# Turning q and k on TensorE's whole array in place of DMA, in an attention and MLP kernel, with a new order of operations

## The chip, the cores and the metric

The kernel runs on one core of a Trainium2 chip. The metric is the device time of one launch in microseconds; the kernel before has a median of 362.71 us in three runs (362.51 to 363.19). TensorE does the matmuls (its weight loads are recorded apart, as PEld), VectorE (DVE), ScalarE (ACT) and GpSimd (POOL) the rest of the arithmetic, SyncE (SP) issues most of the DMAs.

## The reference

Two layers follow each other. The first is attention without softmax over 8 batches of 12 heads, 448 positions and a head width of 64; the second is an MLP over the 3584 tokens, with 768 inputs and 2048 hidden values.

```python
scores = scale * np.matmul(q, k.transpose(0, 1, 3, 2))
attn = np.maximum(scores, 0.0) ** 2 / S
attn_out = np.matmul(attn, v)
x = attn_out.transpose(0, 2, 1, 3).reshape(B * S, H * D)
h = x @ w_in
g = h * (1.0 / (1.0 + np.exp(-1.702 * h)))
return g @ w_out
```

Inputs and outputs are float32; the kernel computes its products in float16 and sums in float32.

## The kernel before

**Units.** The attention is cut into 24 units, three to a batch, each of four heads. For a unit, q and k are loaded, cast to float16, and turned so that the head width lies on partitions (tiles `qT` and `kT`, 128 x 7 x 128). Then come seven steps of scores (`scores`, L147: four matmuls of 64x64 weights and 448 columns, each in a quarter of the array), relu of each half (`relu`, L158 on VectorE, L160 on ScalarE), the square (L166 on ScalarE, or a product on VectorE), the product with v (`attn_v`, L178: 28 quarter-array matmuls), and two copies of the result to the batch's x (`xb`).

**How q and k are turned.** Units 0 to 5 (batches 0 and 1) are turned by TensorE: `trans_pe`, L128, with two matmuls against the identity for each of seven places, one for each half of the array's columns (`tr`), and `trans_evac` copies the PSUM bank to SBUF on VectorE or ScalarE. Of these, unit 0 is loaded as float32 and cast, and units 1 to 5 are cast by the load itself. Units 6 to 23 are loaded as float32 by SP into a single staging buffer for q and one for k (`load`, L96), cast into an order in which seven squares of 128x128 lie side by side (`cast`), and turned by a DMA that SP issues (`trans_dma`, L116). There are two float16 buffers each for q and for k, and three each for `qT` and `kT`.

**The MLP.** Batch 0 goes through the first matrix in a plain way (`m1`, L214, tile `ht`). Batches 1 to 7 use Winograd's form of Strassen's scheme, with seven products in place of eight (`unit_product`, tile `hx`, 224 columns a matmul, at L194), whose intermediate sums are made by VectorE. Snaps and additions collect the quarters in `gf`, then follow the gelu on ScalarE (L201) and its scaling into `ring` (L204, on POOL or VectorE). The second matrix is applied to pairs of 128-token tiles, again with seven products (`pair_product`, tile `ox`, eight matmuls of 384 columns, at L194). A product's bank is copied or added to the output tile `osb` (`pair_snap`, `pair_last`, L366 on VectorE), which `store` (L306) or `store_part` (L313) writes out by DMA.

**What sets the order.** All operations stand in one long list of words, written out by hand, which the function `do` carries out one after the other. Each engine keeps the order of its own operations in that list, and semaphores order operations of different engines. A word names an operation, its unit or block, the engine after a colon and the PSUM banks after an @: `s6.0@2.3` is step 0 of the scores of unit 6 in banks 2 and 3, `Lk9`, `K9:p`, `Rk9` are load, cast on POOL and DMA turn of unit 9's k, `tk2@1` and `ek2` are turn by TensorE and its copy, `u` is a product `hx`, `p` a product `ox`, `h` and `l` the steps that take it from its bank. PSUM has eight banks, which the words name outright.

The core of the turn by DMA, and the end of the list in the old kernel (tiles 26 and 27 are the last pair; a third number of `p` and `l` is a half of the product's columns):

```python
def trans_dma(n, u):
    t = new(f"{n}T", [128, J, 128], F16)
    nc.sync.dma_start_transpose(
        out=t[:, :, :], in_=units[u].pop(n + "16").rearrange("p j a d -> p (j a d)"))
    units[u][n + "T"] = t
...
            "q26.0.0 l26.3.1 q26.0.1:a l26.3.0 q27.1.0 q27.1.1:a l24.6 o24 p26.5 l26.5 p26.6.0 "
            "l26.6.0 p26.6.1 q27.0.1:a q27.0.0 q26.2.0 q26.2.1:a l26.6.1 q26.3.0 q26.3.1:a"
```

Of the kernel before, what the change touches and what calls it, by code (L numbers as in the profile page):

```python
# [8 lines left out]
F32 = mybir.dt.float32  # L9
# [6 lines left out]
def kernel(  # L16
# [77 lines left out]
    def load(n, u):  # L94
        x = new(f"{n}st", [128, 2, S], F32)
        nc.sync.dma_start(out=x, in_=quad(n, u))  # L96
        units[u][n + "st"] = x
# [6 lines left out]
    def cast(n, e, u):  # L104
        x = units[u].pop(n + "st")
        if u == 0:
            c = new(f"{n}16", [128, 2, S], F16)
            copy(e, c, x)
        else:
            c = new(f"{n}16", [128, J, 2, D], F16)  # L110
            copy(e, c.rearrange("p j a d -> p a j d"), x.rearrange("p a (j d) -> p a j d", d=D))
        units[u][n + "16"] = c

    def trans_dma(n, u):
        t = new(f"{n}T", [128, J, 128], F16)
        nc.sync.dma_start_transpose(  # L116
            out=t[:, :, :], in_=units[u].pop(n + "16").rearrange("p j a d -> p (j a d)"))
        units[u][n + "T"] = t
# [4 lines left out]
    def trans_pe(n, p, u):  # L123
        ps = bank(p, "tr", F16)
        x = units[u].pop(n + "16")
        for j in range(J):
            for a in range(2):
                nc.tensor.matmul(  # L128
                    out=ps[64 * a:64 * a + 64, j * 128:(j + 1) * 128],
                    lhsT=x[:, a, 64 * j:64 * j + 64], rhs=ident[:, :], is_transpose=True)  # L130
        units[u][n + "ps"] = ps
# [176 lines left out]
    def store_part(e, p, m, h, i):  # L308
        b, j = divmod(2 * m + i, J)
        r0 = b * S + j  # L310
        c = slice(h * NOUT, (h + 1) * NOUT) if h < 2 else slice(
            NOUT + NOUT // 2 * (h - 2), NOUT + NOUT // 2 * (h - 1))
        (nc.scalar if e == "a" else nc.sync).dma_start(  # L313
            out=out[r0:r0 + 63 * J + 1:J, c], in_=osb[m][64 * i:64 * i + 64, c])
# [30 lines left out]
    def pair_product(e, p, m, n, h=None):  # L345
        c = (0, 1, 0, 1, 0, 0, 1)[n] if h is None else 2 + h
        if n < 2 or (n == 3 and h is not None):
            op[m, c] = bank(p, "ox")
# [4 lines left out]
        mm(op[m, c][:, k], lambda f: a[:, f, :], lambda f: w[:, f, k], HF, n in (0, 1, 3))  # L353

    def pair_snap(e, p, m, n):
        i, c = {0: (0, lo), 2: (0, hi), 4: (1, hi)}[n]
        copy(e, out_tile(m + i)[:, c], op[m, 0][:, 0:NOUT], 1.0 / SC)

    def pair_last(e, p, m, n, h=None):
        i, c = {1: (0, lo), 3: (1, hi), 5: (1, lo), 6: (0, hi)}[n]  # L360
        o = out_tile(m + i)[:, c][:, quarter(h)]
        if n == 5:
            copy(e, o, op[m, 0][:, 0:NOUT], 1.0 / SC)
        else:
            x = op[m, 1 if h is None else 2 + h][:, quarter(h)]
            nc.vector.scalar_tensor_tensor(out=o, in0=x, scalar=1.0 / SC, in1=o,  # L366
                                           op0=ALU.mult, op1=ALU.add)
# [16 lines left out]
    with tc.manual_schedule():  # L384
# [8 lines left out]
        for n in "kq":  # L393
# [3 lines left out]
            two["R" + n] = lambda e, p, u, n=n: trans_dma(n, u)  # L397
# [22 lines left out]
        def zeros(e, p, n):  # L420
# [8 lines left out]
            "z9@0 z1 z1 jq1 z1 z1 jk1 V1 I Lq0 Lk0 z1 z1 z1 Q0:d tq0@1 eq0:a K0:d tk0@2 tq1@3 ek0 "  # L429
            "eq1 s0.5@4.5 jq2 r0.5.1:d r0.5.0 s0.1@6.7 jk2 s0.2@0.1 r0.2.1 r0.1.1:d jq3 s0.0@2.3 "  # L430
            "s0.3@5.4 r0.1.0 r0.2.0:d r0.3.1 r0.3.0:d s0.4@1.7 tk1@6 ek1 s1.6@0.4 s1.4@5.6 jk3 x0.2 "
            "r0.0.0 V0 r0.4.1 r0.0.1 x0.0 r0.4.0 r1.6.0 s0.6@2.7 x0.3 jwa0 s1.0@3.1 r1.6.1 r1.0.1 "
            "tq2@0 x0.5 eq2 s1.5@4.1 r1.4.1 r1.5.0:d s1.3@0.6 jwb0 r1.4.0 r1.5.1 V2 s1.1@4.5 x1.6 "
            "tk2@1 jq4 r1.3.1 jwb2 x1.4 r0.6.1 ek2 r1.1.1 x0.4 jk4 r0.6.0 jwa2 r1.1.0 r1.0.0 tq3@6 "
            "s2.3@7.1 eq3 x0.1 r1.3.0 r2.3.0 s1.2@5.2 r1.2.1 jwa1 x1.1 jwb1 x0.6 tk3@4 r2.3.1 ek3 "
            "jq5 V3 a0@3.6 r1.2.0 jk5 x1.0 jwb3 x1.2 x1.3:a s2.4@0.7 e0.1:a e0.0:a r2.4.0 s3.3@2.1 "
            "x1.5 r3.3.0:d r3.3.1 r2.4.1:d a1@4.5 e1.0:a V4 e1.1:a s2.2@6.3 r2.2.1:d jwa3 s2.5@0.2 "
            "V5 r2.2.0 x2.3 f0.2.0@1 r2.5.0 jo1.0 s2.0@7.4 r2.0.1 s2.1@5.3 r2.1.1 r2.0.0:d r2.5.1 "
            "f0.2.1 jo0.0 x2.2 f0.3.0@6 r2.1.0:d f0.3.1 x2.0 s2.6@0.4 r2.6.1 r2.6.0 s3.1@3.7 r3.1.0 "
            "s3.0@2.5 r3.1.1:d jo1.1 tq4@4 f0.1.0@0 jo0.1 r3.0.0:d eq4 x2.4 x2.6 x2.1:a f0.1.1 "  # L440
            "s3.2@3.7 x2.5:a r3.2.0 a2@2.4 tk4@3 r3.2.1:d r3.0.1 e2.0:a s3.6@7.5 e2.1 ek4 f0.3.2 "
            "r3.6.0:d x3.2 r3.6.1 f0.2.2 g0.3 g0.2 f0.1.2 g0.1 s3.5@2.4 s3.4@3.7 r3.4.0 r3.4.1 "
            "r3.5.0:d s4.4@5.6 r4.4.0:d r4.4.1 v0.2 f0.0.0@1 x3.3 f0.0.1 f0.0.2 f0.8.0@0 g0.0 "
            "s4.5@3.7 r3.5.1:d S0.1 r4.5.0 s4.6@2.5 r4.6.0:d s4.3@6.1 v0.1 f0.8.1 r4.3.0 f0.8.2 "
            "x3.6 r4.6.1 x3.5 x3.0 g0.8 v0.3 s4.2@4.3 r4.2.1 S1.1 s4.1@2.6 r4.2.0 f0.4.0@5 f0.4.1 "
            "f0.5.0@0 f0.4.2 r4.1.0 f0.5.1 x4.6:a x4.2:a G3 v0.8 f0.6.0@3 f0.6.1 r4.3.1:d r4.5.1:d "
            "x3.1 S2.1 f0.6.2 f0.5.2 x4.4 x3.4 f0.7.0@4 g0.6 tq5@2 eq5 S1.2 tk5@1 r4.1.1 g0.4 Lq6 "
            "Lk6 S2.2 ek5:a g0.5 a3@7.3 e3.1:a v0.5 s4.0@2.6 s5.2@5.1 r5.2.1 r4.0.0:d f0.11.0@0 "
            "r4.0.1:d f0.11.1 r5.2.0 f0.11.2 e3.0:a x4.0 x4.5 s5.0@3.1 g0.11 s5.4@2.6 x4.3:a r5.0.1 "
            "s5.5@5.7 f0.7.1 r5.5.1 f0.9.0@0 f0.9.1 f0.9.2 r5.0.0:d f0.7.2 r5.5.0:d s5.3@1.7 r5.4.1 "  # L450
            "x4.1 v0.6 g0.7 a4@3.5 S3.1 s5.1@6.4 r5.3.1 r5.4.0 S2.4 v0.11 v0.7 x5.0:a Q6 r5.3.0:d "
            "s5.6@7.2 S1.3 e4.0 f0.10.0@1 g0.9 S3.2 f0.10.1 v0.9:d r5.6.1 r5.1.1:d u1.2.0@3 S0.3 "
            "f0.15.0@0 x5.3:a f0.14.0@2 r5.1.0 x5.1 f0.15.1 r5.6.0:d v0.4 f0.15.2 f0.14.1 x5.2:a "
            "v0.0 g0.15 f0.10.2 x5.4 T1.1 f0.14.2 u1.3.0@4 g0.10 x5.6:a f0.13.0@6 x5.5 K6 Lk7 "
            "a5@7.0 f0.13.1 S1.4 e4.1:a S3.4 S0.2 S2.3 Lq8 f0.13.2 v0.10:d e5.0:a v0.15:d e5.1:a "
            "Rq6 T1.2 u1.0.0@1 u1.1.0@5 u1.1.1@7 S0.4 t1.0.0 Rk6 g0.14 t1.1.0 T1.3 v0.14:d b1.1.1 "
            "u1.0.2 g0.13 u1.0.1@0 u1.1.2 t1.0.2 u1.0.4 v0.13 b1.0.1 g1.1.1 v1.1.1 W1.1 g1.0.1 "
            "v1.0.1 S3.3 t1.1.2 f0.12.0@2 u1.0.3 t1.0.4 u1.1.4 t1.2.0 T1.4 b1.0.3 u1.1.3 t1.1.4 "
            "u1.3.1@6 g1.0.3 u1.0.6 K7 W2.1 b1.1.3 b1.0.6 u1.0.5 Lk8 f0.12.1 W0.1 v1.0.3 u1.1.6 "
            "u1.2.1@0 g1.0.6 W3.1 b1.1.6 g1.1.3 u1.1.5 b1.2.1 v1.0.6 g1.0.5 u1.2.2 t1.3.0 v1.1.3 "  # L460
            "u1.2.3 g1.2.1 v1.0.5:d v1.2.1 W3.2 t1.2.2 b1.3.1 f0.12.2 W0.2 W0.3 g1.1.6 u1.2.4 g0.12 "
            "p0.0@7 v0.12 t1.2.4 W1.3 Q8:a b1.2.3 v1.1.6 Lq7 u1.2.5 A0.1@0 g1.2.3 W3.3 u1.3.2 Rq8 "
            "A0.2@1 g1.2.5 W2.2 h0.0 u1.2.6 b1.2.6 g1.3.1 v1.3.1 u1.3.3 g1.1.5 W2.4 W1.2 t1.3.2 "
            "p0.1@1 V6 v1.1.5 Rk7 s6.0@2.3 r6.0.0:d A0.3 r6.0.1 v1.2.5 s6.1@0.5 r6.1.0 l0.1 u1.3.4 "
            "t1.3.4 r6.1.1 p0.2 A0.4 x6.0:a s6.2@2.3 r6.2.1 h0.2:d r6.2.0:d s6.4@0.5 r6.4.1 p0.3 "
            "W2.3 b1.3.3 Q7:a W0.4 s6.3@3.2 r6.3.1 x6.1 p0.4 W1.4 K8:p r6.4.0 r6.3.0 W3.4 h0.4 "
            "x6.3:a Rq7 Lk9 l0.3 Lq9 x6.4 u1.3.5 s6.5@5.2 s6.6@0.3 r6.6.1 g1.3.5 r6.6.0 x6.2 u1.3.6 "
            "r6.5.1:d p0.5 r6.5.0 b1.3.6 g1.2.6 s7.0@3.4 l0.5 v1.2.6 r7.0.0:d x6.5 r7.0.1 x7.0 "
            "s7.2@0.2 r7.2.1 s7.4@5.6 r7.4.1 p0.6 s7.1@7.3 s7.6@4.2 r7.4.0 V8 V7 v1.3.5 r7.1.0:d "
            "Rk8 x7.4 x6.6:a r7.1.1 a6@6.5 r7.6.0 s7.3@7.3 K9:p l0.6 Q9 r7.6.1 e6.0:a r7.3.0:d "  # L470
            "r7.3.1 s7.5@4.1 r7.5.0 Lk11 e6.1 p2.0@2 x7.6 r7.2.0 Rk9 s8.5@6.7 s8.4@3.4 x7.1 "
            "s8.2@5.0 r7.5.1 r8.5.1 r8.2.1 Rq9 p2.1@1 A2.1@1 s8.1@7.0 r8.2.0:d r8.4.1 r8.4.0 x7.2 "
            "x7.3 r8.5.0 r8.1.0:d K11:p s8.3@5.4 r8.1.1 x7.5:a r8.3.0 Rk11 r8.3.1:d x8.1:a a7@3.6 "
            "s8.0@7.0 s8.6@5.4 r8.6.0 r8.6.1 A2.2@0 h2.0:d r8.0.1:d Lq10 e7.1:a p2.2 o1 r8.0.0:d "
            "x8.4 e7.0:a x8.0 s9.0@5.4 r9.0.0 x8.3:a x8.2 x8.5 s9.3@0.6 r9.3.1 u2.1.0@7 r9.3.0 h2.2 "
            "r9.0.1 x8.6 a8@3.5 l2.1 Q10 Lk10 o0 s9.1@6.0 r9.1.0 p2.3 A2.3 e8.0:a r9.1.1:d t2.1.0:d "
# [148 lines left out]
```

## Time and profile before

| what | value |
|---|---|
| median of three runs | 362.71 us |
| the profiled execution's own time | 363.36 us |
| its span, first to last instruction | 361.6 us |
| granted TensorE clock | 1.00 |
| turns on TensorE, L128 | 168 matmuls, 7.0 us busy |
| turns by DMA, L116 | 36, each about 1.25 us of issue on SP, 4.0 to 4.3 us to landing |
| moved by DMA | 51.39 MB |

Times and starts are microseconds from the first instruction unless marked ns. A group of instructions has a line, an engine, an operation, the tile it writes and those it reads, and how often. A matmul's recorded duration includes the time in which its result still runs through the array while the next has already begun, so durations of neighbours overlap; the distance from one start to the next tells what a matmul costs in a stream. The chain of work that ended last is followed back from the last instruction, at each step to what released it.

### The profile page before, as it was taken

How to read it: one execution, taken by the hardware profiler on the slowest of the kernel's cores; microseconds unless marked ns; L12 is line 12 of the kernel's file. 1: busy time of each engine (PE TensorE's matmuls, PEld its weight loads, DVE VectorE, ACT ScalarE, POOL GpSimd, SP SyncE). 2: the span in 40 equal slices, each digit the busy share in tenths (PEclk: the TensorE clock that was granted, in tenths of full speed). 3: DMA queues.
4: the chain of work that ended last, by engine and by line, in shares of the span. 5: the costliest groups of instructions: out<-in, count | busy, mean ns of one | idle time of the engine just before them, and what ended most of it. 6: DMA issues, size and time to landing. Idle time of an engine off the chain costs nothing.

```text
span 361.6 us, 9118 instructions
## 1 busy us (share of the span) xinstructions
PE 351.8 (97%) x3600; PEld 240.6 (67%) x3600; DVE 313.2 (87%) x578; ACT 286.0 (79%) x551; POOL 116.9 (32%) x169
## 2 busy tenths in 40 slices
PE   8799999999999999999999999999999999999995
PEld 4444458854579655896568865698579756778663
DVE  3999999999998899899988898989998898674844
ACT  3999898999988998789997799868987898427410
POOL 5735731435135424242244343254121310102000
PEclk9999999999999999999999999999999999999999
DMA  8999999679889999868699625980381101130314
GB/s 178 159 195 205 217 234 240 126 122 229 189 224 268 210 164 182 204 121 199 145 195 172 198 33 86 210 200 0 68 175 46 44 2 45 45 87 2 87 45 133
DMA packets 65388, 51.39 MB, mean 142 GB/s; under 512 B 35776, under 2 KB 62016, under 8 KB 65344
## 3 DMA queue, kind: packets, MB, share of 16 engines
q1 hardware_dynamic: 48336, 36.32, 43.0%
q0 software_dynamic: 16608, 14.09, 26.7%
q8 instruction: 28, 0.46, 0.5%
q10 hardware_dynamic: 400, 0.39, 0.3%
q14 instruction: 16, 0.13, 0.1%
HBM read 45.61 MB, written 11.01 MB: 157 GB/s over the span
## 4 chain that ended last, share of the span: by engine, by line
PE 85%; DMA 6%; DVE 4%; ACT 2%; POOL 2%; issue 1%; POOLq 0%
PE ox L194 34%; PE hx L194 32%; PE sc L147 8%; PE av L178 7%; DMA k<-in_k_dram 3%; DMA q<-in_q_dram 3%; PE ht L214 3%; PE zp L424 1%; DVE at L85 1%; DVE at L158 1%; POOL ring L204 1%; ACT at L160 1%; ACT gf L201 1%; PE tr L128 0%; DVE asum L85 0%
## 5 line engine op out<-in xcount | busy, mean ns | idle before, releaser
L160 ACT ACTIVATE at<-sc 128x448 f16<-128x448 f32 x214 | 104.9, 582 | 7.3 <-PE sc L147 7.2
L204 POOL TENSOR_SCALAR ring<-gf 128x448 f16<-128x448 f32 x94 | 58.0, 617 | 156.1 <-ACT gf L201 152.7
L194 PE MATMUL ox<-wout,ring 128*128 128x384 f16 (+1 forms) x456 | 80.3, 324 | 0.1
L194 PEld LDWEIGHTS <-ring 128*128 128x128 f16 x568 | 53.7, 98 | 35.9 <-issue 6.1
L158 DVE TENSOR_SCALAR at<-sc 128x448 f16<-128x448 f32 x122 | 72.2, 616 | 3.6 <-PE sc L147 2.7
L194 PEld LDWEIGHTS <-win 128*128 128x128 f16 x672 | 64.0, 98 | 6.6 <-issue 3.0
L85 DVE TENSOR_TENSOR at<-at 128x896 f16<-128x896 f16 x102 | 63.1, 644 | 0.3
L166 ACT ACTIVATE at<-at 128x896 f16<-128x896 f16 x66 | 62.7, 969 | 0.8 <-DVE at L158 0.5
L85 DVE TENSOR_TENSOR gf<-hx,gf 128x448 f32<-128x448 f32 x84 | 51.1, 620 | 10.8 <-PE hx L194 4.9
L201 ACT ACTIVATE gf<-gf 128x448 f32<-128x448 f32 x84 | 46.8, 573 | 15.1 <-DVE gf L85 14.9
L194 PE MATMUL hx<-xb,win 128*128 128x224 f16 x504 | 58.0, 259 | 0.0
L147 PE MATMUL sc<-qT,kT 64*64 64x448 f16 x672 | 49.7, 358 | 2.0 <-DVE kT L80 1.4
L194 PEld LDWEIGHTS <-winS 128*128 128x128 f16 x504 | 48.2, 98 | 2.7 <-issue 1.1
L76 ACT ACTIVATE gf<-hx 128x448 f32<-128x448 f32 x59 | 31.4, 542 | 13.2 <-PE hx L194 9.5
L194 PE MATMUL ox<-wT,asum 128*128 128x384 f16 (+1 forms) x232 | 41.0, 321 | 0.7 <-DVE osb L366 0.5
L194 PE MATMUL hx<-T,winS 128*128 128x224 f16 x336 | 39.7, 259 | 0.0
L178 PE MATMUL av<-at,v 64*64 64x448 f16 x672 | 37.1, 350 | 1.2 <-ACT at L160 0.7
L147 PEld LDWEIGHTS <-kT 64*64 64x64 f16 x672 | 18.0, 105 | 25.9 <-issue 18.8
L194 PEld LDWEIGHTS <-asum 128*128 128x128 f16 x232 | 21.4, 98 | 16.8 <-issue 4.4
L366 DVE SCALAR_TENSOR_TENSOR osb<-ox,osb 128x384 f32<-128x384 f32 (+1 forms) x44 | 23.3, 533 | 8.9 <-PE ox L194 6.9
L178 PEld LDWEIGHTS <-v 64*64 64x64 f16 x672 | 19.8, 106 | 14.0 <-issue 2.8
L80 POOL CAST q<-qst 128x896 f16<-128x896 f32 x13 | 13.4, 1028 | 39.6 <-DMA qT<-q 14.5
(57 smaller groups left out, 363.3 us busy)
## 6 DMA issues: line engine op xcount, KB each, us to landing
out_dram<-osb SPq DMA_DIRECT2D x52, 192.0 KB, 3.4
qst<-in_q_dram SPq DMA_DIRECT2D x19, 448.0 KB, 4.9
kst<-in_k_dram SPq DMA_DIRECT2D x19, 448.0 KB, 4.4
v<-in_v_dram POOLq DMA_DIRECT2D x24, 224.0 KB, 5.7
win<-in_moe_w_in_dram POOLq DMA_DIRECT2D x8, 384.0 KB, 12.3
wout<-in_moe_w_out_dram POOLq DMA_DIRECT2D x4, 768.0 KB, 20.6
q<-in_q_dram POOLq DMA_DIRECT2D x5, 224.0 KB, 5.3
k<-in_k_dram POOLq DMA_DIRECT2D x5, 224.0 KB, 5.9
```

Source lines behind the costliest of these rows:

```text
L76: nc.scalar.activation(out=o, in_=i, func=AF.Copy)
L80: eng[e].tensor_copy(out=o, in_=i)
L85: eng[e].tensor_tensor(out=o, in0=x, in1=y, op=op)
L147: nc.tensor.matmul(out=sc[a][c, 0:S], lhsT=st["kT"][r, j, c], rhs=st["qT"][r, :, c], start=True, stop=True)
L158: nc.vector.tensor_scalar(out=o, in0=i, scalar1=0.0, scalar2=None, op0=ALU.max)
L160: nc.scalar.activation(out=o, in_=i, func=AF.Relu)
L166: nc.scalar.activation(out=at, in_=at, func=AF.Square)
L178: nc.tensor.matmul(out=av[s][64 * a:64 * a + 64, 0:S], lhsT=v16[r, a, 64 * j:64 * j + 64], rhs=at[r, a, :], start=(j == 0), stop=(j == J - 1))
L194: nc.tensor.matmul(out=o, lhsT=lhs(i), rhs=rhs(i), start=start and i == 0, stop=i == n - 1, skip_group_check=True)
L201: nc.scalar.activation(out=o, in_=i, func=AF.Gelu_apprx_sigmoid, scale=1.0 / SC)
L204: eng[e].tensor_scalar(out=o, in0=i, scalar1=SC, scalar2=1.0, op0=ALU.mult, op1=ALU.mult)
L366: nc.vector.scalar_tensor_tensor(out=o, in0=x, scalar=1.0 / SC, in1=o, op0=ALU.mult, op1=ALU.add)
```

## The change

Every unit's q and k are now turned by TensorE. A unit that was cast by an engine (unit 0, and 6 to 23) lies in the order of seven squares of 128x128, and `trans_pe` turns each with one matmul on the whole array; units 1 to 5 keep their two matmuls for each place. `trans_dma` and its 36 words are gone, and 36 words of turn and 36 of copy have come: 17 of these copies are on ScalarE and 19 on VectorE. The casts of units 6 to 23 and other operations that can be done on more than one engine are divided in another way.

For the last pair, product 5 is the one that is split in two halves, each in a bank of its own, in place of products 3 and 6. Its bank is therefore taken in parts: products 0, 2 and 4 are copied out by a `pair_snap` (`h26.5`), and the two halves are added to that. A new function, `from_bank`, copies or adds according to whether that part of the output tile has been begun. All words stand in a new order.

```diff
-        if u == 0:
-            c = new(f"{n}16", [128, 2, S], F16)
-            copy(e, c, x)
-        else:
-            c = new(f"{n}16", [128, J, 2, D], F16)
-            copy(e, c.rearrange("p j a d -> p a j d"), x.rearrange("p a (j d) -> p a j d", d=D))
-        units[u][n + "16"] = c
-
-    def trans_dma(n, u):
-        t = new(f"{n}T", [128, J, 128], F16)
-        nc.sync.dma_start_transpose(
-            out=t[:, :, :], in_=units[u].pop(n + "16").rearrange("p j a d -> p (j a d)"))
-        units[u][n + "T"] = t
+        c = new(f"{n}16", [128, J, 2, D], F16)
+        copy(e, c.rearrange("p j a d -> p a j d"), x.rearrange("p a (j d) -> p a j d", d=D))
+        units[u][n + "16"] = c.rearrange("p j a d -> p (j a d)")
...
         x = units[u].pop(n + "16")
         for j in range(J):
+            if len(x.shape) == 2:
+                nc.tensor.matmul(out=ps[:, j * 128:(j + 1) * 128],
+                                 lhsT=x[:, j * 128:(j + 1) * 128], rhs=ident[:, :],
+                                 is_transpose=True)
+                continue
             for a in range(2):
...
+    def from_bank(e, x, t, c):
+        o = out_tile(t)[:, c]
+        part_done = (t, c.start) in begun
+        begun.update((t, i) for i in range(c.start, c.stop, NOUT // 2))
+        if part_done:
+            nc.vector.scalar_tensor_tensor(out=o, in0=x, scalar=1.0 / SC, in1=o,
+                                           op0=ALU.mult, op1=ALU.add)
+        else:
+            copy(e, o, x, 1.0 / SC)
...
-            "Lk6 S2.2 ek5:a g0.5 a3@7.3 e3.1:a v0.5 s4.0@2.6 s5.2@5.1 r5.2.1 r4.0.0:d f0.11.0@0 "
...
+            "p26.2 l24.6 A26.4 o24 A26.3 p26.3 h26.2 p26.4 l26.3 p26.6 h26.4:d h26.5 q27.1.1:a "
+            "q27.1.0 p26.5.0@4 q26.0.1:a l26.6 p26.5.1@3 q26.1.1:a q26.1.0 l26.5.0 q27.2.1:a "
+            "q27.2.0 l26.5.1 q27.3.1:a q27.3.0"
```

## The prediction

> **What bounds the kernel now.** I read the page's busy shares first, then the table by stretches, then the chain of work that ended last, and last the timeline of TensorE, for the distance from one group of matmuls to the next.
>
> ```profile
> PE 351.8 (97%) x3600; PEld 240.6 (67%) x3600; DVE 313.2 (87%) x578; ACT 286.0 (79%) x551; POOL 116.9 (32%) x169
> PEclk9999999999999999999999999999999999999999
> ```
>
> TensorE is busy 97% of the span at the full granted clock. A matmul's busy time reaches past the start of the next one, so 97% does not say how much room is left. For that I take distances between starts, from the chain:
>
> ```profile
> 229.86 1.32 PE av L178 x28
> 231.18 0.38 PE sc L147 x8
> 231.56 1.41 PE ox L194 x8
> 232.97 8.05 PE hx L194 x84
> 241.02 1.30 PE ox L194 x8
> ```
>
> So hx takes 8.05/84 = 0.0958 us each, ox 1.30/8 = 0.1625, av 1.32/28 = 0.047, sc 0.38/8 = 0.0475. Whole program: hx 1176 x 0.0958 = 112.7; ox 768 x 0.1625 = 124.8, and 32 half-width ones 2.6; av 672 x 0.047 = 31.7; sc 672 x 0.0475 = 31.9; ht 96 x 0.189 (eight in 1.51 us in the chain) = 18.1; turns 12 x 0.42 (below) = 5.0; the warming zp 5.3. Sum 332.1 of 361.6: 29.5 us of TensorE's span carry no streaming.
>
> They lie in three places. Up to 50 us the groups of that stretch (70 ht, 168 sc, 140 av, 168 tr, 16 zp, 3 hx) sum to 38.4, so 11.6 are empty. After the last matmul 4.4 us pass (the last DVE step starts at 357.22). The middle has the other 13.5. Most of that is visible in the timeline:
>
> ```profile
> 215.07 2.77 PE L194 MATMUL ox<-wout,ring 128*128 128x384 f16 x16
> 217.77 0.76 PE L147 MATMUL sc<-qT,kT 64*64 64x448 f16 x12
> 218.47 1.47 PE L194 MATMUL ox<-wT,asum 128*128 128x384 f16 x8
> ```
>
> Sixteen ox should take 2.60 and take 2.70; twelve sc should take 0.57 and take 0.70. Each change between whole-array and quarter-array matmuls costs about 0.11 us. The order has 87 of them behind 50 us: 9.6 of the 13.5 us. These gaps are too short to hold a turn, which needs 0.4 us. So behind 50 us TensorE is the bound, and what is added there lengthens the span nearly in full. The other engines, by stretches (columns: us, then busy us and count of PE, PEld, DVE, ACT, POOL, clock, DMA share, GB/s):
>
> ```profile
> 0.00:50.00 50.00, 45.53 (x565) 23.55 (x566) 42.95 (x80) 41.60 (x85) 29.27 (x44) 1.00 1.14 198
> 50.00:100.00 50.00, 49.70 (x504) 32.60 (x501) 49.28 (x93) 47.32 (x93) 16.80 (x24) 1.00 0.94 185
> 100.00:300.00 200.00, 199.42 (x2062) 143.29 (x2055) 183.14 (x335) 173.22 (x328) 66.54 (x95) 1.00 0.68 141
> 300.00:361.60 61.60, 57.18 (x482) 41.15 (x480) 37.79 (x73) 23.83 (x49) 4.28 (x7) 1.00 0.26 65
> ```
>
> VectorE and ScalarE have no room from 50 to 100, about 43 us together from 100 to 300, and much room after that.
>
> **The change, part by part.**
>
> *Turns added to TensorE.* Units 6 to 23 each turn q and k: 36 tiles of seven matmuls, 252 more. The nearest row is the old turn of units 0 to 5, two half-array matmuls for each of the seven places:
>
> ```profile
> 38.70 0.54 PE L214 MATMUL ht<-xb,win 128*128 128x448 f16 x2
> 39.17 0.58 PE L128 MATMUL tr<-ident,q 128*64 128x128 f16 x14
> 39.59 0.56 PE L128 MATMUL tr<-ident,k 128*64 128x128 f16 x14
> ```
>
> Fourteen start over 0.42 us, so a pair that turns 128 columns costs 0.06. A whole-array turn streams the same 128 columns once, so I take 7 x 0.06 = 0.42 a tile: 36 x 0.42 = 15.1 us. Lower bound: ox streams 384 columns in 0.1625, so 128 in 0.054; 252 x 0.054 = 13.7. Upper bound: the page's weight loads of 128x128 last 98 ns each; if these can't overlap one another, 252 x 0.098 = 24.7. Hx starts every 0.0958 with such a load each, which doesn't decide it; the half-wide loads (110 ns in the group of line 128) do overlap, since pairs start every 0.06. Hence 15.1. Unit 0 goes from 14 halves to 7 whole ones: nothing. Nothing hides the 15.1, as TensorE streams without a break there.
>
> The Trainium skill speaks against the change more strongly than this row. "TensorE: Matmul & The Clock Gate", Part 4, gives a turn on TensorE about 275 ns within a kernel and says that the clock gate doesn't count it as busy; 252 x 0.275 would be 69 us and a time near 433. Here a turn does last 219 ns in its group, but the next pair starts 0.06 us later, and the clock stays at 9 in the slices with turns. The same page ("Back-to-back issue gap") puts a stream of weight load and matmul at about 81 ns for 128 columns: 252 x 0.081 = 20.4 us instead of 15.1. I stay with the row and keep 20.4 inside the range.
>
> *Changes of the array's shape.* Between whole-array and quarter-array work the new order has 118 changes (whole-array turns counted as whole), the old one 109: 9 x 0.11 = +1.0. Below: 0. Above: if a turn is itself a change on both sides of its 29 visits, 29 x 0.22 = 6.4. I take 1.0, since from ht into a half-array turn (38.70 to 39.17, two ht being 0.38) only 0.09 is lost.
>
> *Evacuation added.* Each turn leaves PSUM by a copy: 17 of the 36 on ScalarE at 0.93 us (the one kT row there has 0.938) = 15.8, 19 on VectorE at 0.62 = 11.8. Other words change sides (relu, squares, snaps, casts), and the net by the same rows is about +13 on ScalarE and +14 on VectorE. From 100 on, 24 copies (18.6 us) fit the 43 free ones. From 50 to 100 there is no room: 12 copies, 9.3 us, are 4.7 for each engine, beside 12 x 0.42 = 5.0 that TensorE gains in the same stretch. The stretch grows by the larger, and I add 0.5 for what doesn't overlap. Below: 0, if they overlap; above: +4.7. Each turn also holds a PSUM bank for its matmuls and copy, about 1.5 us, 54 of 8 x 361 bank-microseconds. A turn waits in TensorE's queue for its cast, and the matmuls queued behind wait with it, and for those ScalarE and VectorE. In the order the cast stands about 5 us of TensorE work or more ahead of its turn, but for unit 7's q (1.8) and unit 6's q (directly ahead, near 41 us, cast by VectorE in about 0.65): 0 to 1.5 us, of which I take 0, because TensorE is not yet full there.
>
> *Removed: 36 turns by DMA*, and with them 36 issues of about 1.25 us on SP's queue, their packets, and the waits for them. The waits that the profile shows are of POOL (casts of q waited 14.5 us for the turn to free the buffer) and of SP (40 us for sc to free kT and qT). TensorE, which sets the end, shows no wait for them. POOL is busy 32%, so that gives 0; what is late next on SP are the loads, which still wait for the single staging buffers to be cast. Bounds: 0 to -1.
>
> *The last pair.* The order ends with product 5 in two halves in place of product 6; half-products are 196 in both. One ScalarE copy more lies beside matmuls. The end is again eight half-width matmuls, one 0.36 us VectorE step and a 48 KB store. 0, within 0.5 either way.
>
> *The start.* The same loads in nearly the same order on SP and POOL (one v load earlier), and the first 50 us are held by loads, DVE and ACT. 0, within 3 either way.
>
> Sum on the profiled execution's own time, 363.36: + 15.1 + 1.0 + 0.5 = 380.0. The median, 362.71, is 0.65 lower: 379.3.
>
> **The rivals.**
>
> *The weight loads set the pace of the turns.* For it: 98 ns a load, and the 81 ns rule. Against: the overlap in the old turns. 363.4 + 24.7 + 1.5 = 389.6, median 389; by 81 ns 384.6. Chance 0.12.
>
> *VectorE and ScalarE become the bound between 50 and 100, and the copies come on top.* For it: 49.28 and 47.32 of 50. Against: TensorE grows there as well, which gives them that time. 380.0 + 4.7, median 384. Chance 0.12.
>
> *Faster: the new order empties TensorE's gaps.* The place is the first 50 us, where 11.6 are empty, and the middle with 13.5. The added 16.6 are paid only if more than that vanishes: all of the start's and 6 of the middle give 363.4 + 16.6 - 17.6 = 362.4, median 361.7. For it: the chain before 37 us runs over a load of q (9.83) and one of k (11.79), which another order might avoid. Against: DVE and ACT fill that stretch too, and the order has more changes of shape, not fewer. Faster 0.06, the same 0.02, partly (up to 373.5) 0.04.
>
> **How the numbers follow.** The likeliest case, 0.64, is 379.3, by its bounds 375 to 384. The range is 373.5 to 387: it takes in the VectorE case and the 81 ns case, and leaves out the gap case and the full weight-load case. Some 0.2% is what a measurement of this kernel can tell from no change. Slower 0.92, same 0.02, faster 0.06.
>
> **What would show it.** Right: turns of whole tiles starting about 0.06 us apart, 36 groups of seven at 0.42; TensorE's part of the span longer by 15 us; no DMA turns; DVE near 327 and ACT near 299 busy; the stretch behind the last hx as long as before. Wrong: turns 0.08 to 0.1 apart (first rival); gaps in front of relu-fed matmuls between 50 and 110 (second); the first hx, at 49.8 now, much earlier (third); TensorE waiting for casts or for a free bank.

## The result, and the profile after

The changed kernel takes 374.8 us (373.97 to 374.81, three runs) against 362.71: a ratio of 1.0323, 95% interval 1.0296 to 1.035. It is slower, as forecast, 4.5 us below the predicted 379.3 and inside the range. The profiled execution took 374.80 us (span 373.0), 11.4 more than the one before.

First the page: busy time of the engines, TensorE's clock, the DMA queue to which the turns belonged (packets, MB, share of 16 engines), and the shares of the chain that ended last.

```profile
PE 365.6 (98%) x3830; PEld 252.9 (68%) x3830; DVE 321.5 (86%) x602; ACT 297.3 (80%) x568; POOL 114.3 (31%) x164
...
PEclk9999999999999999999999999999999999999999
...
q1 hardware_dynamic: 14928, 28.06, 25.7%
...
PE 95%; DVE 3%; ACT 1%; issue 0%
```

TensorE is as full as before, and its granted clock stays at 9 in every slice. The last line, the chain, read "PE 85%; DMA 6%; DVE 4%; ACT 2%; POOL 2%; issue 1%; POOLq 0%" before; now it runs over nothing but TensorE once the start is past. Such shares are weak evidence where two paths are nearly equally long: the same order with another end (the last experiment, 1 us slower) has "PE 86%; DVE 8%; ACT 2%; DMA 1%; issue 1%; SPq 0%; ACTq 0%". The queue's packets fall from 48336 to 14928. The stretches again, with the same columns (the last two are divided at 310 us in place of 300):

```profile
0.00:50.00 50.00, 47.19 (x561) 24.50 (x562) 42.96 (x82) 43.84 (x91) 27.82 (x43) 1.00 1.16 201
50.00:100.00 50.00, 49.99 (x545) 34.62 (x544) 48.89 (x94) 46.87 (x89) 17.12 (x23) 1.00 0.78 182
100.00:310.00 210.00, 210.00 (x2247) 152.45 (x2248) 187.62 (x348) 181.85 (x343) 64.98 (x92) 1.00 0.38 95
310.00:373.00 63.00, 58.38 (x482) 41.35 (x480) 42.08 (x82) 24.73 (x47) 4.38 (x7) 0.99 0.26 64
```

From 50 to 310 us TensorE is recorded busy without a break. Now the turns, first their group (durations in ns as min/median/max), then the chain around some of them:

```profile
L117 PE MATMUL tr<-ident,q x133: 219/219/230, 6.2 to 274.3; 128*128 128x128 f16 x133
```

```profile
186.58 1.41 PE ox L188 x8
187.99 0.78 PE tr L117 x14
188.77 3.90 PE ox L188 x24
192.67 0.50 PE sc L141 x8
193.17 1.32 PE av L172 x28
194.49 0.38 PE sc L141 x8
194.87 1.41 PE ox L188 x8
196.28 1.73 PE hx L188 x18
198.00 0.39 PE tr L117 x7
198.40 0.57 PE hx L188 x6
```

A tile of seven turns takes 0.39 us and two take 0.78: 0.0558 us a turn, though each is recorded as 219 ns. Before and behind a turn nothing is lost: the 24 ox behind it take 3.90, exactly 24 x 0.1625, while the eight ox behind sc take 1.41 in place of 1.30. A whole-array turn among whole-array matmuls is thus no change of the array's shape.

**Where the 11.4 us come from.** I price every matmul by its distance in a stream (hx 0.0958, ox 0.1625, ht 0.189, av and sc 0.0472, a turn 0.0558) and call the rest of the elapsed time between starts empty. The warming zp is priced as ox, and the 1.1 us ahead of the first matmul belong to the last row; so the table has 13.6 empty us up to 50 us in the kernel before, where the prediction had 11.6.

| part | before | after | difference |
|---|---|---|---|
| streaming, all matmuls | 329.1 | 343.2 | +14.1 |
| empty up to 50 us | 13.6 | 11.8 | -1.8 |
| empty from 50 us to the last matmul | 13.2 | 12.1 | -1.1 |
| the rest (start, end, rounding) | | | +0.2 |
| sum | | | +11.4 |

In the third row about 0.10 us for each change between quarter and whole array is included. There are 87 of them before and 99 after, so by this price the changes cost 1.2 more, and the other waits fall from about 4.5 to 2.2.

### The profile page after: what moved, and what is told of

Its sections match the earlier page's. It is cut to its first block, busy times and chain, and to the rows that moved or that the text cites. A ratio compares the mean times of both kernels' runs of the same rounds, so it can differ in the third digit from the quotient of the medians.

```text
span 373.0 us, 9514 instructions
## 1 busy us (share of the span) xinstructions
PE 365.6 (98%) x3830; PEld 252.9 (68%) x3830; DVE 321.5 (86%) x602; ACT 297.3 (80%) x568; POOL 114.3 (31%) x164
## 4 chain that ended last, share of the span: by engine, by line
PE 95%; DVE 3%; ACT 1%; issue 0%
PE ox L188 35%; PE hx L188 30%; PE sc L141 10%; PE av L172 8%; PE ht L208 5%; PE tr L117 4%; PE zp L426 1%; DVE at L85 1%; DVE at L152 1%; PE tr L122 1%; ACT at L154 1%; DVE kT L80 0%; DVE qT L80 0%; DVE osb L357 0%; DVE wT L417 0%
## 5 line engine op out<-in xcount | busy, mean ns | idle before, releaser
L154 ACT ACTIVATE at<-sc 128x448 f16<-128x448 f32 x229 | 112.2, 567 | 10.6 <-PE sc L141 9.9
L198 POOL TENSOR_SCALAR ring<-gf 128x448 f16<-128x448 f32 x87 | 53.7, 617 | 151.0 <-ACT gf L195 144.0
L188 PE MATMUL ox<-wout,ring 128*128 128x384 f16 x448 | 80.3, 326 | 0.0
L152 DVE TENSOR_SCALAR at<-sc 128x448 f16<-128x448 f32 x107 | 63.9, 617 | 5.8 <-PE sc L141 5.6
L85 DVE TENSOR_TENSOR at<-at 128x896 f16<-128x896 f16 x107 | 65.5, 636 | 1.7 <-ACT at L154 1.6
L160 ACT ACTIVATE at<-at 128x896 f16<-128x896 f16 x61 | 57.7, 960 | 0.5
L188 PE MATMUL hx<-xb,win 128*128 128x224 f16 x504 | 57.0, 259 | 0.0
L195 ACT ACTIVATE gf<-gf 128x448 f32<-128x448 f32 x84 | 47.2, 578 | 11.5 <-DVE gf L85 11.3
L76 ACT ACTIVATE gf<-hx 128x448 f32<-128x448 f32 x60 | 31.8, 541 | 13.4 <-PE hx L188 11.4
L188 PE MATMUL ox<-wT,asum 128*128 128x384 f16 x224 | 40.6, 327 | 0.0
L172 PE MATMUL av<-at,v 64*64 64x448 f16 x672 | 36.2, 350 | 0.1
L188 PEld LDWEIGHTS <-asum 128*128 128x128 f16 x224 | 20.8, 98 | 16.6 <-issue 3.4
L78 ACT ACTIVATE osb<-ox 128x384 f32<-128x384 f32 x26 | 13.1, 503 | 19.6 <-PE ox L188 16.8
L172 PEld LDWEIGHTS <-v 64*64 64x64 f16 x672 | 20.4, 107 | 11.6 <-issue 1.5
```

Source lines behind the costliest of these rows:

```text
L76: nc.scalar.activation(out=o, in_=i, func=AF.Copy)
L85: eng[e].tensor_tensor(out=o, in0=x, in1=y, op=op)
L152: nc.vector.tensor_scalar(out=o, in0=i, scalar1=0.0, scalar2=None, op0=ALU.max)
L154: nc.scalar.activation(out=o, in_=i, func=AF.Relu)
L160: nc.scalar.activation(out=at, in_=at, func=AF.Square)
L172: nc.tensor.matmul(out=av[s][64 * a:64 * a + 64, 0:S], lhsT=v16[r, a, 64 * j:64 * j + 64], rhs=at[r, a, :], start=(j == 0), stop=(j == J - 1))
```

## The experiments

My theory A was: behind 50 us TensorE is full, the change costs the streaming of 252 turns, and the new order gives back 2.6 us of TensorE's gaps. Theory B: a good part of the cost is the 36 copies on VectorE and ScalarE and the waits they bring. Theory C: the new order is by itself the slower one. Theory D, added on the way: the cost is a sum of a half from each.

Each kernel's time stands beside runs of the kernel before on the same chip: 362.75 us in the first set, 362.78 in the second, 363.08 in the third.

**The turns done twice.**

```diff
-                nc.tensor.matmul(out=ps[:, j * 128:(j + 1) * 128],
-                                 lhsT=x[:, j * 128:(j + 1) * 128], rhs=ident[:, :],
-                                 is_transpose=True)
+                for _ in range(2 if u > 5 else 1):
+                    nc.tensor.matmul(out=ps[:, j * 128:(j + 1) * 128],
+                                     lhsT=x[:, j * 128:(j + 1) * 128], rhs=ident[:, :],
+                                     is_transpose=True)
```

> The changed kernel with each of the 252 whole-array turns of units 6 to 23 done twice in a row into the same place; nothing else is added. Theory A (TensorE has no room behind 50 us, a turn costs 0.056 us): 374.8 + 14.1 = 388.9. If a part of a turn is hidden by gaps at places where TensorE waits for VectorE and ScalarE (theory B), the second copy of it is hidden as well, and the time stays below 385.

Measured: 388.56 us, ratio 1.0698 (1.0679 to 1.0716), 13.8 more than the changed kernel. Theory A holds for what is added to TensorE: each turn is paid in full, at 0.055 us, at the places where the turns stand.

**The copies done twice.**

```diff
-        copy(e, t, units[u].pop(n + "ps")[:, 0:J * 128].rearrange("p (j c) -> p j c", j=J))
+        ps = units[u].pop(n + "ps")[:, 0:J * 128].rearrange("p (j c) -> p j c", j=J)
+        for _ in range(2 if u > 5 else 1):
+            copy(e, t, ps)
```

> The changed kernel with each of the 36 copies of a turned tile from PSUM done twice in a row on its engine (17 on ScalarE, 19 on VectorE, 27.6 us more in all). Theory A: 375 to 377, because only the twelve copies between 50 and 110 us (9.3 us, 4.7 on each engine) find no room. Theory B (the copies are a good part of what the change costs): 12 us or more on top, 385 to 388.

Measured: 388.25 us, 1.0683 (1.0659 to 1.0706), 13.5 more. Here my theory A failed and B's number came, to within 0.3. The second copies add 27.7 us of busy time, 12.4 on VectorE and 15.3 on ScalarE, and the time grows by as much as one engine got. Its chain:

```profile
PE 67%; DVE 20%; ACT 6%; issue 3%; DMA 1%; POOL 1%; DVEq 0%; POOLq 0%; ACTq 0%
```

VectorE and ScalarE now hold 26% of the chain, against 4% in the changed kernel; and TensorE's empty time behind 50 us, priced as above, is about 26 us in place of 12. So the changed kernel stands at two limits at once, and what is added to either lengthens it. That calls for taking away in place of adding.

**Without turns, without copies, without both.** The three edits, each for units above 5; the kernel without both has the second edit as well as the third:

```diff
+            if u > 5 and j > 0:
+                continue
...
+            copy(e, t, ps[:, 0:128].unsqueeze(1).to_broadcast([128, J, 128]))
```

> The changed kernel with six of the seven turns of each tile of units 6 to 23 left out (216 of 252 matmuls); the copy of the tile stays, with the same number of elements, and repeats the one square that was turned, so the scores of those units are of other numbers. Theory A (TensorE's streaming alone is the price): 374.8 - 216 x 0.056 = 362.7. Theory B, put anew after the doubled copies cost 13.5 us (TensorE is full, and VectorE with ScalarE are full as well up to about 300 us, so that either of the two additions alone lengthens the time by most of it): 369 to 374. Theory D (the price is a sum of two halves): 367 to 369.

```diff
+        if u > 5:
+            units[u].pop(n + "ps", None)
+            units[u][n + "T"] = last[n]
+            return
...
```

> The changed kernel with all turns on TensorE, but without the 36 copies: the scores of units 6 to 23 read unit 5's turned tiles. This takes 27.6 us off VectorE and ScalarE. Theory A: 373.5 to 374.8, as TensorE's work is unchanged. Theory B: 372 to 374.8 as well. Theory D: 367 to 369.

```diff
-            two["t" + n] = lambda e, p, u, n=n: trans_pe(n, p, u)
+            two["t" + n] = lambda e, p, u, n=n: trans_pe(n, p, u) if u < 6 else None
```

> The changed kernel without turns and without copies for units 6 to 23, whose scores read unit 5's turned tiles: what the new order costs with q and k turned by nobody. Theories A and B: 374.8 - 14.1 = 360.7, with up to 1.5 less, as nothing waits for a turn. Theory C (the new order is the slower one by itself): 362.7 or more.

| kernel | us | ratio to before | chain, by engine |
|---|---|---|---|
| turns and copies (the change) | 374.8 | 1.0323 (1.0296 to 1.035) | PE 95%, DVE 3%, ACT 1% |
| turns alone | 374.18 | 1.032 (1.0294 to 1.0345) | PE 86%, DVE 9%, ACT 1% |
| copies, one turn in seven | 370.47 | 1.0208 (1.0178 to 1.0237) | PE 65%, DVE 18%, ACT 9% |
| neither | 368.5 | 1.016 (1.0134 to 1.0187) | PE 69%, DVE 21%, ACT 5% |

The second row is what theories A and B both expected; it rules out D. Taking 27.6 us off VectorE and ScalarE gives 0.6 us, which is not clear of noise (373.8 to 375.35 against 373.97 to 374.81). The third lies in B's range: without 12.1 us of turns the time falls by only 4.3. But the fourth shows that the copies are not the reason. With them gone as well the time falls by only another 2.0, and the 36 turns that the kernel of the third row still does stream for as much (36 x 0.0558). What takes over is the order itself: TensorE's empty time behind 50 us, priced as above, is about 19 us in the third row and 21 in the fourth, against 12.1 in the changed and 13.2 in the old one.

The fourth row surprised me: the new order without any turning is 5.7 us slower than the old kernel, where I expected 2 faster. That is theory C's number. Its stretches and, from the list of waits, who waited for whom (us in total, times, longest):

```profile
50.00:100.00 50.00, 47.73 (x484) 31.40 (x482) 49.63 (x92) 42.64 (x85) 21.39 (x23) 1.00 0.80 183
100.00:310.00 210.00, 207.50 (x2090) 144.87 (x2088) 185.71 (x339) 175.79 (x338) 65.27 (x93) 1.00 0.38 95
```

```profile
ACT gf L200 <- DVE gf L85: 14.6, 19, 2.7
ACT gf L76 <- PE hx L193: 12.9, 11, 2.0
ACT at L159 <- PE sc L146: 11.0, 21, 1.2
```

VectorE is full from 50 to 100 (49.63 of 50) while ScalarE is busy for 42.64; over the whole span ScalarE's three waits are 11.3, 11.4 and 9.9 in the changed kernel. The -1.8 and -1.1 of the table thus don't mean that the new order is a better one in itself. Without turns it is the slower one; in the changed kernel its waits lie where the turns cover them. Which of its words bring the waits stays open.

**The turns in the old order.** To see what the turns cost without an order made for them, I put them into the old words, with the old end. Each `R` word gave way to a `t` at or near its place, in a bank that is free there, and an `e` some words later.

```diff
-            ... Rq8 ... Rk7 ...
+            ... tq8@2 ... eq8:a ... tk7@5 ... ek7:a ...
```

> The old kernel with its old order and old last pair, in which each turn by DMA is replaced by the whole-array turn on TensorE at or near its place, in a PSUM bank that is free there, and by a copy some words later on the engine that the new order uses for it. Theory A: 362.7 + 14.1 = 376.9, and 0 to 3 more, as these words were put in by hand. Theory B (VectorE and ScalarE have no room either in an order that wasn't made for the copies): 380 to 390, with TensorE waiting for relu and squares in the attention's stretches.

Measured: 392.81 us, 1.0844 (1.0806 to 1.0881), 30.0 more than before, and 18 more than the changed kernel; that is far above A's range and 2.8 above B's. Two further kernels keep the old order and its DMA turns, and add at the same places either turns of the identity that nobody reads, or one such turn and a copy to a spare tile.

```diff
+    def spare_turn(n, p, u):
+        ps = spare[n, u] = bank(p, "tr", F16)
+        for j in range(7):   # 1 in the kernel with copies
+            nc.tensor.matmul(out=ps[:, j * 128:(j + 1) * 128], lhsT=ident[:, :],
+                             rhs=ident[:, :], is_transpose=True)
...
+        copy(e, heap, ps[:, 0:128].unsqueeze(1).to_broadcast([128, J - 1, 128]))
```

> The old kernel, with its DMA turns, and besides 252 turns on TensorE of the identity into a free bank, at the places of the kernel with the old order and turns by TensorE; nobody reads them. Theory A (TensorE is full in the old order): 362.7 + 14.1 + about 1 for changes of shape = 377 to 378.5. Where TensorE's waits in the old order are room that a turn can use: 370 to 374.

> The old kernel, with its DMA turns, and besides one turn of the identity and one copy from PSUM of 128 x 768 elements (six repeats of it) to a spare tile for each of the 36 tiles, at the same places and on the same engines as in the kernel with the old order and turns by TensorE: 17 on ScalarE, 19 on VectorE, about 24 us in all; nobody reads them. If VectorE and ScalarE are hidden behind TensorE in the old order: 363 to 367 (the 36 turns are 2 us). Theory B (they are full too): half of 24 and the 2, 373 to 377.

Measured: 381.63 us with turns (1.0502, 1.0482 to 1.0523), 18.6 more than before; 390.98 with copies (1.0751, 1.0722 to 1.0779), 27.9 more. The first lies 3 us above A's range. It is 14.1 of streaming and 4.5 of waits, which TensorE's own list of waits names:

```profile
PE tr L143 <- DVE at L169: 2.2, 3, 1.1
PE tr L143 <- ACT at L171: 2.1, 4, 0.7
```

A turn that I put behind scores waits for a relu to free its bank, 4.3 us in seven cases: that is my placing, not the turn. So TensorE had no room for turns in the old order either.

The copies cost more than either theory allowed: some 24 us of them, 2 of turns, and 27.9 in the time. In the profiled execution the empty time behind 50 us grows by 24, so the copies are paid nearly whole and not by half. Another 1.5 us lie in the first 50 us, where none of these copies stands and the granted clock was 0.97 (the run with the highest clock, 0.996, took 388.8). TensorE's waits are put down to the copies themselves for 10.8 us, in 14 cases; that the rest comes through a relu or a square that stands behind a copy on its engine is argued, not shown. The two costs are no sum: turns alone are 18.6 more, copies alone 27.9, and both, there without the DMA turns, 30.0. How much a better placing would save, these runs don't say; in the changed kernel the copies cost about 0.6.

**DMA turns in the new order.**

```diff
...
-            two["t" + n] = lambda e, p, u, n=n: trans_pe(n, p, u)
-            two["e" + n] = lambda e, p, u, n=n: trans_evac(n, e, u)
+            two["t" + n] = lambda e, p, u, n=n: trans_dma(n, u) if u > 5 else trans_pe(n, p, u)
+            two["e" + n] = lambda e, p, u, n=n: None if u > 5 else trans_evac(n, e, u)
```

> The new order and the new end, but q and k of units 6 to 23 are turned by DMA again: each is issued by SP at the place where the turn by TensorE stood, and the copies from PSUM are gone. Theory A (the change costs the streaming of 252 matmuls on TensorE, 36 x 0.39 = 14.1 us, and the new order by itself gives back 2.6 us of TensorE's gaps): 374.8 - 14.1 = 360.7, up to 1 more where scores wait for a DMA that lands late. Theory B (a sizeable part of the cost is the 36 copies on VectorE and ScalarE, and the waits that they bring): clearly below, 356 to 359. Theory C (the new order is by itself the slower one): 362.7 or more.

Measured: 407.06 us, 1.1213 (1.118 to 1.1246). Of the theories only the open end of C takes that in, and not for its reason. The waits of SP's queue, of POOL and of TensorE, and TensorE's clock:

```profile
SPq L114 <- PE sc L146: 53.5, 8, 14.6
```

```profile
POOL k L80 <- DMA kT<-k: 43.4, 6, 11.7
PE hx L193 <- DVE gf L85: 13.6, 3, 5.3
PE sc L146 <- DVE at L157: 9.2, 3, 5.2
```

```profile
PEclk9999999999967997998999999889999999999999
```

Moved to the places of the PE turns, a DMA turn waits at the head of SP's queue for scores to free `kT` (14.6 us in one case), the loads stand behind it, POOL's casts wait for the landing, and at last TensorE waits over 5 us at a time and its clock is granted at 0.6 to 0.8 for a while. This kernel says nothing of the new order's worth, for which I had meant it; it says that the places of the PE turns are too late for a DMA turn.

**Turns on half arrays.**

```diff
+            if len(x.shape) == 2 and u > 5:
+                for a in range(2):
+                    c = 128 * j + 64 * a
+                    nc.tensor.matmul(out=ps[64 * a:64 * a + 64, j * 128:(j + 1) * 128],
+                                     lhsT=x[:, c:c + 64], rhs=ident[:, :], is_transpose=True)
+                continue
```

> The changed kernel with each whole-array turn of units 6 to 23 done as two turns on the two halves of the array's columns, side by side, as units 1 to 5 do it: 504 matmuls in place of 252. The streaming is the same if the two halves run together (a pair starts every 0.056 us). Theory A with shape changes priced by any change of the array's use: some 29 visits, each with about 0.1 us in and out towards whole-array neighbours and none saved towards quarter-array ones, 374.8 + 4 to 6 = 379 to 381. If half-array use costs no change: 374.8. If the whole array is what makes a turn cheap, and halves run one after the other: 389.

Measured: 380.21 us, 1.0471 (1.0453 to 1.0488), 5.4 more than whole-array turns. Its chain, where the changed kernel had 0.39 and 0.57:

```profile
201.85 0.51 PE tr L119 x14
202.36 0.68 PE hx L194 x6
```

The halves stream together, but 0.12 and 0.11 us are lost going in and out, as theory A said. Doing the turn on the whole array is worth those 5.4 us.

**The start.** The old kernel with two words changed:

```diff
-            ... v0.2 f0.0.0@1 ... v0.1 f0.8.1 ...
+            ... v0.2:d f0.0.0@1 ... v0.1:d f0.8.1 ...
```

> The old kernel with two words changed: the scaling of blocks 2 and 1 of batch 0 into the ring moves from POOL, where it stands behind the issues of the loads of w_out, to VectorE. In the old profile ScalarE waits 1.76 us near 38.5 us for POOL's scaling to free a gf buffer, and TensorE then loses some 1.1 us between 40 and 50. Theory A on the start (this is where the new order is 1.8 us better in the first 50 us): 361.6 to 362.0. If VectorE, which gets 1.2 us more there, is the limit: 362.7 to 363.5.

In the old kernel ScalarE waits here for POOL, which has 3.5 us of issues of `wout` loads ahead of the scaling (timeline of the kernel before):

```profile
37.00 0.87 POOL L376 DMA_DIRECT2D wout<-in_moe_w_out_dram  x1 [0.32 <-DMA k<-in_k_dram]
37.95 4.54 POOL L204 TENSOR_SCALAR ring<-gf 128x448 f16<-128x448 f32 x4
```

```profile
40.23 0.54 ACT L201 ACTIVATE gf<-ht 128x448 f32<-128x448 f32 x1 [1.76 <-POOL ring L204]
```

With the edit that wait is gone:

```profile
37.96 0.54 ACT L201 ACTIVATE gf<-ht 128x448 f32<-128x448 f32 x1
```

Measured: 362.21 against 363.08 us, 0.9975 (0.9959 to 0.9991): 0.9 faster, between the two ranges. In the profiled execution TensorE's empty time up to 50 us is 11.9 in place of 13.6, as in the changed kernel (11.8), which has one of these scalings on VectorE. But the kernel with the turns in the old order, whose first 50 us are the old kernel's, has 12.7, so some 0.9 of such a difference can be chance. The wait is worth 0.9 us of time; that all of the start's 1.8 come from it is not shown.

**The old end in the new kernel.**

```diff
-            ... A26.3 p26.3 h26.2 p26.4 l26.3 p26.6 h26.4:d h26.5 ... l26.6 ...
+            ... A26.3 p26.3.1@3 p26.3.0@4 h26.2 p26.4 l26.3.1 l26.3.0 p26.5 h26.4:d ... l26.5 ...
```

> The changed kernel with the old last pair: products 3 and 6 of tiles 26 and 27 in halves and product 5 whole, and the stores that go with it; all else is as in the changed kernel. Every theory: 374.8, within 0.5; if the new end gives something, 375.5 or more.

Measured: 375.88 us, 1.035 (1.033 to 1.037), 1.1 more than the changed kernel and just past what I allowed. The changed kernel ran beside other runs of the kernel before, and the intervals of the two ratios overlap. In this kernel product 5 stands ahead of `h26.4` and so enters a second quarter of the pair's output as well. The profiled spans differ by 1.0; 0.7 of it comes behind the last VectorE step (4.9 us, against 4.2 in the changed kernel and 4.0 in the old one), where the last stores, which begin 1.6 us later than in the changed kernel, are still being issued. So the new end is not shown to give anything against the old one in its own place; at most it does against the one that I set in.

## Why the prediction was right

**Turns on TensorE, 15.1 predicted.** Measured 14.1: 0.0558 us a turn, not 0.06. The old tile of fourteen halves, from which I took 0.42, held 0.02 for the change of shape on entry: its second pair starts 0.077 us behind its first and the others 0.056 apart, and the half-array kernel shows the same. Doubling the turns cost 13.8. The first rival, turns paced by weight loads at 98 or 81 ns, is out. The Trainium skill ("TensorE: Matmul & The Clock Gate", Part 4) gives about 275 ns; one turn is recorded here as 219 ns, and neither is what a turn costs in a stream of matmuls. The clock stayed at 9 through all 38 whole-array tiles.

**Changes of shape, +1.0 predicted.** Counted behind 50 us they are 12 more, 1.2 us by this trace; and a whole-array turn is none among whole-array neighbours.

**Copies, +0.5 predicted, hidden because TensorE grows beside them.** That held: without copies the time is 0.6 lower, not clear of noise, and with the turns left out the copies cost 2.0 at most. The busy times grew less than forecast, VectorE's by 8.3 and ScalarE's by 11.3 in place of 14 and 13. But the reason was incomplete. I had read the room of VectorE and ScalarE from a stretch of 200 us, where 43 us looked free. The copies of this order fit into it; the doubled ones, at the same places, found almost none of it. The second rival's mechanism is thus real, one step away: it decides when the order is not made for the copies (30 us in the old order) or when more is added.

**The start, 0 predicted within 3.** Measured -1.8 in one pair of traces, of which 0.9 is shown to come from a wait of ScalarE for POOL. It stood in the list of waits, and I did not look for it because it is not TensorE's.

**Waits behind 50 us, taken as unchanged.** They fell by 2.3. With 1.0 of the turns, 0.5 of the copies (which have no row of their own) and 1.8 of the start, less 0.2 for the changes of shape and 0.2 in the rest, this makes 5.2, which is the difference between 380.0 and 374.8.

**The order itself, taken as neutral.** Here luck helped the number. Without turns and copies the new order is 5.7 us slower than the old kernel, and put onto it the turns cost 5.7 us (6.3 with their copies), not 15.1, as they fill its waits. The sum came out because the changed kernel's last limit is TensorE again, as the prediction assumed; that its order has a second limit just below, on VectorE and ScalarE, was not foreseen.

**The third rival** (gaps that empty) was real in kind, and paid 4.1 us of the 16.6 that it needed.

**Removal of the DMA turns, 0 to -1.** Nothing in these runs shows a gain from it, and no run isolates it.

## What to carry to other kernels

Where TensorE streams without a break and stays the last limit, work that is moved to it costs its streaming in full, and that can be computed from the distances between starts in a neighbouring stream, not from durations. The same kernel can be just as full on the engines that feed TensorE: double one suspect at a time, and take it away as well, since a sum over busy time shows neither limit. An order belongs to the work that it was made for: 18 us lie between the same turns put into the old order by hand and into an order made for them.

## What the hardware showed that was not expected

A whole-array turn between matmuls of the same shape costs 0.0558 us with its weight load, and nothing at its edges; the same turn on two halves loses about 0.1 us on each side towards a whole-array neighbour (5.4 us over 36 tiles).
